# Where a kernel splits its tokens and stores them, and how it sums its last rows

## The chip, the cores and the metric

The kernel runs on one core of a Trainium2 chip. The metric is the device time of one execution in microseconds (us). Before the change it is 602.17 us, the median of three runs (601.52 to 602.39).

## What is computed

A sequence of 2048 tokens of 512 channels goes through two branches, and a gate per token mixes them.

```python
g = sigmoid((x * gate_w).sum(-1, keepdims=True))
a = ssm(x)                                    # long convolution per channel, plus x * D_skip
b = ((x @ w_gate) * (x @ w_up)) @ w_down      # bilinear GLU, 1792 hidden channels
out = g * a + (1 - g) * b
```

In `ssm` the convolution's kernel K (2048 values per channel) is a sum of 128 complex exponentials, made from the parameters; the reference then multiplies Fourier transforms of K and x.

## The kernel before, in words

**Precision.** The GLU's matmuls take operands in fp32r, a form of fp32 with fewer bits. So each operand is *split* into a high part (a cast on ScalarE) and a low part (what is left, a subtraction on VectorE), and each product is three matmuls: low by high, high by low, high by high (`THREE`, line 525). A split is `split` (411).

**GLU.** The 1792 hidden channels are 14 blocks f of 128, in four groups of 3, 3, 4 and 4 blocks (line 24). The 2048 tokens are four columns of 512. For each group the columns are run through: 0 to 3 in the first group, 3 to 0 in the second, and so on to and fro, so that the column at the turn stays in place (`glu`, 630). For a column and a block, `hidden` (543) makes two products of 512 tokens, `pg` and `pu`, each of 4 x 3 matmuls; ScalarE copies pg out as `h`, VectorE multiplies pu by it, and the result is split into `hh` and `hl`. For each of the column's four rows of 128 tokens, `down` (570) then multiplies by the down weights (`dhi`, `dlo`) of the group's blocks into a bank `y`, of which there are two; `evacuate` (581) copies y out, scaled by 1 - g, and writes it to the output in the first group or adds it to the output by an accumulating DMA of GpSimd in the later ones.

**Tokens.** A column's tokens are four tiles `xs` of [128, 2, 512], high and low part, out of five buffers (`tokens`, 515). In the first group they are loaded unsplit into `raw` (two buffers, which the weights go through too, in a fixed order of turns), split into xs (ScalarE and VectorE), and stored split, 512 KB a tile, to `xs_d` in device memory. In the second, third and fourth group each column after the first is loaded from `xs_d`, 512 KB a tile. The column at the turn isn't loaded.

**Weights.** The first group's weights are split by ScalarE and VectorE, as are the down weights of the last. Of the others the high part is cast, and the low part is made by a negated copy and an accumulating DMA from the source (`rest`, 431).

**Convolution.** In 16 blocks of 32 channels, VectorE and ScalarE make tables of complex powers, and one step on TensorE (`k_block`, 1014, written `k<-v,x` in the trace) makes K of these channels from them. After every four blocks, a quarter q of the channels is transformed (`transforms`, 1312): two steps `k<-kt,w1k_t`, then for four parts T a second step (`m_second`, 1131) and a product on VectorE (`m_product`), after each two of them an inverse step (`m_inverse`, 1189), and at last `m_last` (1231, `k<-in,w_t` or `k<-x,w_t`). Between these steps the data go through device memory (`su_d`, `sk_d`, `y_d`). The transform of u (`u_part`, 664) and the gate come at the start, with a load of 1 MB of u for each of four parts.

**The end.** Rows of column 0 come last in the last group. Their output so far is loaded once into `sums` (tile kt in the trace). `ends` (599) adds for each of the four rows g times the convolution (two small operations, for the last two quarters of the channels), then the evacuated y, and stores the row with 256 KB. The fourth row's y goes to a buffer of raw instead of acc, so that four rows have room.

**Order.** The functions don't issue: they add tasks with an engine, an estimated length, what they read and write, and a rank. `Work.run` (263) then goes through all tasks as a planner: of those that can start it takes the one with the earliest start, then the lowest rank, with a model of engines and of one memory bus (300 bytes a ns). The instructions are issued on each engine in this order, for the whole kernel, and each engine works strictly in it. Nearly all instructions have the line of the planner's issuing helper, L119, in the profile.

Of the kernel before, what the change touches and what calls it, by code (L numbers as in the profile page):

```python
# [14 lines left out]
ALU = mybir.AluOpType  # L15
# [3 lines left out]
P = 128  # L19
L, D, N, F = 2048, 512, 128, 1792  # L20
KT = D // P
# [4 lines left out]
LAST = 3 if len(GROUPS) % 2 else 0  # L26
# [138 lines left out]
class Work:  # L165
# [27 lines left out]
    def add(self, engine, us, fn, r=(), w=(), rank=1, after=0.0, dma=0, hold=(), rows=(), many=0):  # L193


        task = Task(len(self.tasks), engine, us, fn, rank, after, dma)
        task.rows, task.many = rows, many
        self.tasks.append(task)
        clash = lambda p, q: p is None or q is None or p == q
        split = lambda x: x if isinstance(x, tuple) else (x, None)  # L200
        for tile, part in map(split, r):
            task.deps.update(t for p, t in tile.writers if clash(p, part))
        for tile, part in map(split, w):
            task.deps.update(t for p, t in tile.writers + tile.readers if clash(p, part))
        for tile, part in map(split, r):
            tile.readers.append((part, task))
        for tile, part in map(split, w):
            tile.writers.append((part, task))
        for tile, _ in map(split, [*r, *w, *hold]):
            if tile.pool and tile not in task.tiles:  # L210
                task.tiles.append(tile)
                tile.users.append(task)
        task.deps.discard(task)
        return task
# [105 lines left out]
def gated_mix_kernel(  # L320
# [16 lines left out]
    pe, dve, act, sp, pool_q = (InOrder(tc, e) for e in (nc.tensor, nc.vector, nc.scalar, nc.sync, nc.gpsimd))  # L337
    uv = u.rearrange("(p r) d -> p r d", r=NR)
    ov = out.rearrange("(p r) d -> p r d", r=NR)
    work = Work()  # L340
    add = work.add
# [12 lines left out]
    m_su, m_sk, m_y, m_out, m_xs, m_turn = (work.memory() for _ in range(6))  # L354
# [5 lines left out]
    def new(pool, tag, shape, dtype=F32, bufs=1, loose=False):  # L360
        return work.tile(pools[pool], tag, shape, dtype, bufs, loose)
# [14 lines left out]
    ngate = const.tile([P, NR], F32, name="ngate")  # L376
    m_gate = work.memory()
# [27 lines left out]
    def load(key, src, rank=0):  # L405
        if key in raws:
            return
        t = raws[key] = new("glu", "raw", [P, D], bufs=2)
        add("sp", 0.42, lambda: sp.dma_start(t.t, src), w=[t], dma=256, rank=rank)

    def split(hi, lo, s, key):

        t = raws[key]
        t, k = t if isinstance(t, tuple) else (t, None)
        src = lambda: t.t if k is None else t.t[:, k]
        got = t if k is None else (t, k)
        s, z = s if isinstance(s, tuple) else (s, s)
        ph, pl = (hi, s), (lo, z)
        at = lambda x, s: x.t if s is None else x.t[:, s] if hi is lo else x.t[:, s * D : (s + 1) * D]
        add("act", 0.62, lambda: act.copy(at(hi, s), src()), r=[got], w=[ph], rank=0)  # L420
        add(
            "dve", 0.69,
            lambda: dve.tensor_tensor(out=at(lo, z), in0=src(), in1=at(hi, s).bitcast(F32), op=ALU.subtract),
            r=[got, ph], w=[pl], rank=0,
        )
# [49 lines left out]
    def weights(fs):  # L475
        for f in fs:
            ws[f] = [new("glu", n, [P, 2 * D], F32R, SLOTS) for n in ("whi", "wlo")]
            if f == 0:
                for kt in range(KT):
                    first_split(kt)  # L480
                    if kt + 1 < KT:
                        tokens(0, 0, kt + 1)
                continue
            for c in range(2):
                load(("w", f, c), wts[f][:, c * D : (c + 1) * D])
                if f in GROUPS[0]:
                    split(*ws[f], c, ("w", f, c))
                else:
                    high(ws[f][0], c, ("w", f, c))
            if f not in GROUPS[0]:  # L490
                rest(*ws[f], wts[f][:, : 2 * D], 2)
# [23 lines left out]
    def tokens(gi, ci, kt):  # L515

        x = xs[kt] = new("glu", "xs", [P, 2, D], F32R, 5)
        if gi:
            add("sp", 0.42, lambda: sp.dma_start(x.t.bitcast(F32), xs_d[ci, kt]), r=[(m_xs, (ci, kt))], w=[x], dma=512, rank=0)
            return  # L520
        load(("x", gi, ci, kt), xT[kt * P : (kt + 1) * P, ci * D : (ci + 1) * D])
        split(x, x, (0, 1), ("x", gi, ci, kt))
        add("sp", 0.42, lambda: sp.dma_start(xs_d[ci, kt], x.t.bitcast(F32)), r=[x], w=[(m_xs, (ci, kt))], dma=512, rank=2)

    THREE = ((1, 0), (0, 1), (0, 0))
# [53 lines left out]
    ending = []  # L579

    def evacuate(gi, ci, r, y):
        t = 4 * ci + r
        final = gi == len(GROUPS) - 1 and ci == LAST
        acc = new("glu", "raw", [P, D], bufs=2) if final and r == 3 else new("glu", "acc", [P, D], bufs=3)
        add(
            "act", 0.69, lambda: act.activation(acc.t, y.t, AF.Copy, scale=ngate[:, t : t + 1]),
            r=[y, (m_gate, ci)], w=[acc], rank=0,
        )
        if final:
            ending.append((r, acc))  # L590
        elif gi == 0:
            add("sp", 0.42, lambda: sp.dma_start(ov[:, t, :], acc.t), r=[acc], w=[(m_out, t)], dma=256)
        else:
            add(
                "pool", 0.95, lambda: pool_q.dma_start(ov[:, t, :], acc.t, accum_op=ALU.add),
                r=[acc, (m_out, t)], dma=640, rows=[t],
            )

    def ends():

        t0 = 4 * LAST
        sums = new("tab", "kt", [P, 4, D])
        add(
            "sp", 0.42, lambda: sp.dma_start(sums.t, ov[:, t0 : t0 + 4, :]),
            r=[(m_y, (KT - 1, 0))], w=[sums, *((m_out, t0 + r) for r in range(4))], dma=1024, rows=range(t0, t0 + 4),
        )
        for r, acc in ending:
            t = t0 + r
            for q, (fin, parts) in late["fin"].items():
                add(  # L610
                    "dve", 0.25,
                    lambda r=r, q=q, t=t, fin=fin: dve.scalar_tensor_tensor(
                        sums.t[:, r, P * q : P * q + P], fin.t[:, 4 * (LAST % 2) + r], gate[:, t : t + 1],
                        sums.t[:, r, P * q : P * q + P], op0=ALU.mult, op1=ALU.add,
                    ),
                    r=[*parts, (m_gate, LAST)], w=[(sums, (r, q))], rank=0,
                )
            add(
                "dve", 0.69,
                lambda r=r, acc=acc: dve.tensor_tensor(  # L620
                    out=sums.t[:, r], in0=acc.t, in1=sums.t[:, r], op=ALU.add
                ),
                r=[acc], w=[(sums, (r, q)) for q in range(KT - 2, KT)], rank=0,
            )
            add(
                "sp", 0.42, lambda r=r, t=t: sp.dma_start(ov[:, t, :], sums.t[:, r]), r=[(sums, (r, q)) for q in range(KT - 2, KT)], w=[(m_out, t)],
                dma=256, rank=-1,
            )

    def glu():  # L630
        order = [(gi, ci) for gi in range(len(GROUPS)) for ci in (range(4) if gi % 2 == 0 else range(3, -1, -1))]
        tokens(0, 0, 0)
        weights(GROUPS[0])
        down_weights(GROUPS[0])
# [728 lines left out]
    for b in range(NB):  # L1363
# [10 lines left out]
        if b % 4 == 3:  # L1374
            transforms(b // 4)
    ends()

    work.run()
# [53 lines left out]
```

## Time and profile before

| | |
|---|---|
| median of three runs | 602.17 us |
| profiled execution | 601.78 us |
| its span, first to last instruction | 600.0 us |
| TensorE busy | 585.8 us |
| VectorE busy | 512.3 us |
| ScalarE busy | 401.0 us |
| moved by DMA | 137.33 MB |

The profile is of one execution. Busy time of TensorE counts a matmul from its start to its modelled end, and matmuls overlap, so a busy TensorE need not be at its peak. In a row of a time line come the start in us, the length in us, engine, line, operation, tile written <- tiles read, shape, count, and in brackets the idle time of the engine before it with what ended it. PE is TensorE, DVE VectorE, ACT ScalarE, POOL GpSimd, SP SyncE; SPq is the queue on which SyncE issues DMAs. In a row of a group stand the busy time and the mean ns of one, then the idle time before. In a row of DMA issues stand the count, the KB of each and the median us to landing. In a row of waits stand the total us, the number of times, and the longest.

### The profile page before, as it was taken

To read this page: it belongs to the slowest core of one execution; us is meant where nothing else is said; L and a number is where in the kernel's file an instruction comes from. 1 tells how busy PE (TensorE), PEld (TensorE's weight loads), DVE (VectorE), ACT (ScalarE), POOL (GpSimd) and SP (SyncE) were. 2 spreads that over 40 slices of the span, in tenths; PEclk is the share of its full clock that TensorE was granted. 3 is DMA by queue.
4 is the path that set the end of the run, shared out by engine and by line. 5 is a ranking of instruction groups with operands and counts; after the bars stand their busy time and mean duration, and the time that the engine had idled before them with its cause. 6 is when DMAs were issued, how large, how long until landed. Compare 5 with 4: busy or idle time off the path is not lost.

```text
span 600.0 us, 15878 instructions
## 1 busy us (share of the span) xinstructions
PE 585.8 (98%) x6500; PEld 443.4 (74%) x6500; DVE 512.3 (85%) x811; ACT 401.0 (67%) x893; POOL 128.9 (21%) x191
## 2 busy tenths in 40 slices
PE   8899999999999999999999999999999999999996
PEld 5657777777877787887777877866878777767674
DVE  6999999999998997999999999978999933486525
ACT  5279787999678479967959764979984423433522
POOL 0011212221204131310133301104353023201111
PEclk9989999999999999999999999999999999999998
DMA  8899979699869699996959945999999569959976
GB/s 276 314 357 340 336 281 338 187 207 253 232 175 227 166 241 248 195 229 163 302 135 266 215 129 171 226 250 239 182 203 260 95 159 355 244 153 264 279 141 122
DMA packets 71867, 137.33 MB, mean 229 GB/s; under 512 B 7156, under 2 KB 35828, under 8 KB 69364
## 3 DMA queue, kind: packets, MB, share of 16 engines
q1 hardware_dynamic: 47476, 88.21, 45.9%
q0 software_dynamic: 23904, 47.98, 40.4%
q8 instruction: 51, 0.84, 0.6%
q10 hardware_dynamic: 416, 0.13, 0.1%
q14 instruction: 20, 0.16, 0.1%
HBM read 81.25 MB, written 55.05 MB: 227 GB/s over the span
## 4 chain that ended last, share of the span: by engine, by line
PE 79%; DVE 8%; ACT 6%; DMA 5%; issue 1%; ACTq 0%; DVEq 0%
PE y L119 22%; PE pu L119 21%; PE pg L119 21%; PE k L119 15%; DMA raw<-in_wts 4%; DVE x L119 2%; DVE y L119 1%; DVE v L119 1%; ACT ts L119 1%; ACT whi L119 1%; DMA y<-in_xT 1%; ACT L119 1%; DVE h L119 1%; DVE t L119 1%; DVE xs L119 1%
## 5 line engine op out<-in xcount | busy, mean ns | idle before, releaser
L119 PE MATMUL pg<-xs,whi 128*128 128x512 f32 x448 | 139.2, 392 | 1.0 <-DVE xs L119 0.7
L119 PE MATMUL pu<-xs,whi 128*128 128x512 f32 x448 | 138.7, 391 | 0.0
L119 PEld LDWEIGHTS pg<-xs,whi 128*128 128x128 f32 x448 | 84.5, 189 | 20.0 <-ACT whi L119 2.0
L119 PEld LDWEIGHTS pu<-xs,whi 128*128 128x128 f32 x448 | 84.4, 188 | 17.1
L119 PE MATMUL y<-dhi,hl 128*128 128x512 f32 x224 | 90.5, 404 | 2.2 <-DVE x L119 1.1
L119 PE MATMUL pu<-xs,wlo 128*128 128x512 f32 x224 | 90.1, 402 | 0.9 <-issue 0.5
L119 PE MATMUL pg<-xs,wlo 128*128 128x512 f32 x224 | 90.1, 402 | 0.8 <-ACT whi L119 0.5
L119 PE MATMUL y<-dlo,hh 128*128 128x512 f32 x224 | 87.5, 391 | 1.3 <-DVE dlo L119 1.3
L119 PE MATMUL y<-dhi,hh 128*128 128x512 f32 x224 | 87.4, 390 | 0.0
L119 POOL DMA_DIRECT2D out<-acc x44 | 38.4, 954 | 184.8 <-ACT acc L119 173.8
L119 ACT COPY ev<-k 128x512 f32<-128x512 f32 x112 | 59.2, 595 | 15.7 <-PE k L119 15.6
L119 ACT CAST hh<-h 128x512 fp32r<-128x512 f32 x56 | 34.7, 620 | 43.3 <-DVE h L119 43.2
L119 ACT ACTIVATE acc<-y,ngate 128x512 f32<-128x512 f32 x63 | 42.8, 686 | 30.6 <-PE y L119 28.2
L119 DVE TENSOR_TENSOR h<-pu,h 128x512 f32<-128x512 f32 x56 | 38.6, 689 | 23.0 <-PE pu L119 22.2
L119 PEld LDWEIGHTS y<-dhi,hl 128*128 128x128 f32 x224 | 42.0, 188 | 21.7 <-issue 6.2
L119 PEld LDWEIGHTS pu<-xs,wlo 128*128 128x128 f32 x224 | 42.1, 188 | 19.2 <-issue 9.8
L119 PEld LDWEIGHTS pg<-xs,wlo 128*128 128x128 f32 x224 | 42.0, 188 | 19.1 <-issue 6.8
L119 ACT COPY h<-pg 128x512 f32<-128x512 f32 x56 | 33.1, 590 | 29.7 <-PE pg L119 27.8
L119 PEld LDWEIGHTS y<-dlo,hh 128*128 128x128 f32 x224 | 42.1, 188 | 9.5 <-DVE dlo L119 1.7
L119 PEld LDWEIGHTS y<-dhi,hh 128*128 128x128 f32 x224 | 42.1, 188 | 9.1
L119 DVE TENSOR_TENSOR hl<-h,hh 128x512 fp32r<-128x512 f32 x56 | 38.5, 687 | 8.4 <-ACT hh L119 8.4
L119 POOL DMA_DIRECT2D su_d<-ev x32 | 17.3, 549 | 90.2 <-ACT ev L119 90.2
(127 smaller groups left out, 1015.7 us busy)
## 6 DMA issues: line engine op xcount, KB each, us to landing
xs<-xs_d SPq DMA_DIRECT2D x36, 512.0 KB, 7.8
out<-acc POOLq DMA_DIRECT2D x44, 256.0 KB, 7.1
raw<-in_wts SPq DMA_DIRECT2D x36, 256.0 KB, 5.2
xs_d<-xs SPq DMA_DIRECT2D x16, 512.0 KB, 7.1
su_d<-ev POOLq DMA_DIRECT2D x32, 256.0 KB, 5.3
y_d<-ts SPq DMA_DIRECT2D x14, 512.0 KB, 6.5
in<-su_d POOLq DMA_DIRECT2D x24, 256.0 KB, 8.4
sk_d<-ev SPq DMA_DIRECT2D x6, 1024.0 KB, 6.2
```

Source lines behind the costliest of these rows:

```text
L119: got = getattr(self.engine, name)(*args, **kw)
```

## The change

Two edits. First, `tokens`: in the first group only column 3 is stored split. Columns 2, 1 and 0 are loaded unsplit again in the second group, split once more, and stored to `xs_d` there; column 3 isn't loaded in the second group, as it is the one at the turn. The third and fourth group read `xs_d` as before. In Python `gi > (ci < 3)` is `gi > 1` for columns 0 to 2 and `gi > 0` for column 3.

Second, the end: of the last column's four rows, the last two are not copied out of PSUM by ScalarE. Their bank y is read by the final sum on VectorE, which scales it by 1 - g in the same operation. The first two rows' sum is the same operation with a scale of 1.0. The fourth row's sum and store are cut into halves of 256 channels, the second half stored on ScalarE's queue. The convolution's share lies in the second half, and the parts that the planner knows are named accordingly.

```diff
@@ tokens
-        if gi:
+        if gi > (ci < 3):
             add("sp", 0.42, lambda: sp.dma_start(x.t.bitcast(F32), xs_d[ci, kt]), ...)
             return
         load(("x", gi, ci, kt), xT[kt * P : (kt + 1) * P, ci * D : (ci + 1) * D])
         split(x, x, (0, 1), ("x", gi, ci, kt))
+        if gi == 0 and ci < 3:
+            return
         add("sp", 0.42, lambda: sp.dma_start(xs_d[ci, kt], x.t.bitcast(F32)), ..., dma=512, rank=2)
@@ evacuate
-        acc = new("glu", "raw", [P, D], bufs=2) if final and r == 3 else new("glu", "acc", [P, D], bufs=3)
+        if final and r > 1:
+            ending.append((r, y))
+            return
+        acc = new("glu", "acc", [P, D], bufs=3)
@@ ends
-                    r=[*parts, (m_gate, LAST)], w=[(sums, (r, q))], rank=0,
+                    r=[*parts, (m_gate, LAST)], w=[(sums, (r, 1))], rank=0,
                 )
-            add(
-                "dve", 0.69,
-                lambda r=r, acc=acc: dve.tensor_tensor(
-                    out=sums.t[:, r], in0=acc.t, in1=sums.t[:, r], op=ALU.add
-                ),
-                r=[acc], w=[(sums, (r, q)) for q in range(KT - 2, KT)], rank=0,
-            )
-            add(
-                "sp", 0.42, lambda r=r, t=t: sp.dma_start(ov[:, t, :], sums.t[:, r]), ...
-                dma=256, rank=-1,
-            )
+            for n, cs in enumerate((slice(0, D // 2), slice(D // 2, D)) if r == 3 else (slice(0, D),)):
+                part = [(sums, (r, k)) for k in (range(2) if r < 3 else (n,))]
+
+                def total(r=r, t=t, acc=acc, cs=cs):
+                    scale = 1.0 if r < 2 else ngate[:, t : t + 1]
+                    dve.scalar_tensor_tensor(
+                        sums.t[:, r, cs], acc.t[:, cs], scale, sums.t[:, r, cs], op0=ALU.mult, op1=ALU.add
+                    )
+
+                add("dve", 0.42 if r == 3 else 0.69, total, r=[acc, (m_gate, LAST)], w=part, rank=0)
+                e, q = ("act", act) if n else ("sp", sp)
+                add(
+                    e, 0.42, lambda r=r, t=t, cs=cs, q=q: q.dma_start(ov[:, t, cs], sums.t[:, r, cs]), r=part,
+                    dma=128 if r == 3 else 256, rank=-1,
+                )
```

More of the change, by code (lines that the diff above doesn't have):

```diff
@@ L615, in ends @@
                     ),
-                    r=[*parts, (m_gate, LAST)], w=[(sums, (r, q))], rank=0,
+                    r=[*parts, (m_gate, LAST)], w=[(sums, (r, 1))], rank=0,
                 )
-            add(
-                "dve", 0.69,
-                lambda r=r, acc=acc: dve.tensor_tensor(
-                    out=sums.t[:, r], in0=acc.t, in1=sums.t[:, r], op=ALU.add
-                ),
-                r=[acc], w=[(sums, (r, q)) for q in range(KT - 2, KT)], rank=0,
-            )
-            add(
-                "sp", 0.42, lambda r=r, t=t: sp.dma_start(ov[:, t, :], sums.t[:, r]), r=[(sums, (r, q)) for q in range(KT - 2, KT)], w=[(m_out, t)],
-                dma=256, rank=-1,
-            )
+            for n, cs in enumerate((slice(0, D // 2), slice(D // 2, D)) if r == 3 else (slice(0, D),)):
[11 more added lines that the diff above has]
+                )
     def glu():
```

## The prediction

> **What bounds the kernel now.** I read the page first, then the busy time by stage (stages cut at 30, 45, 105, 225, 405 and 480 us), then the time line of the stages with loss, and last the waits and the transfers.
>
> ```profile
> span 600.0 us, 15878 instructions
> ...
> PE 585.8 (98%) x6500; PEld 443.4 (74%) x6500; DVE 512.3 (85%) x811; ACT 401.0 (67%) x893; POOL 128.9 (21%) x191
> ```
>
> ```profile
> core 0: us, PE busy (x) PEld busy (x) DVE busy (x) ACT busy (x) POOL busy (x), PEclk, DMA share, GB/s
> 0.00:15.00 15.00, 12.64 (x41) 8.17 (x42) 9.95 (x32) 8.90 (x16) 0.96 (x25) 1.00 0.85 276
> 15.00:30.00 15.00, 12.61 (x55) 9.90 (x54) 14.39 (x31) 4.18 (x7) 0.00 (x0) 1.00 0.84 314
> 30.00:45.00 15.00, 13.88 (x71) 8.12 (x69) 14.95 (x30) 11.01 (x38) 1.97 (x4) 0.89 0.96 356
> 45.00:105.00 60.00, 59.82 (x430) 44.13 (x431) 58.79 (x104) 48.45 (x104) 13.18 (x25) 1.00 0.89 324
> 105.00:225.00 120.00, 119.27 (x1325) 93.15 (x1328) 114.68 (x172) 94.13 (x216) 29.67 (x39) 1.00 0.84 211
> 225.00:405.00 180.00, 179.84 (x2303) 138.25 (x2286) 168.21 (x245) 138.00 (x305) 35.60 (x43) 1.00 0.87 211
> 405.00:480.00 75.00, 74.30 (x874) 57.93 (x875) 72.35 (x110) 54.90 (x128) 24.99 (x31) 1.00 0.92 196
> 480.00:600.00 120.00, 113.46 (x1428) 83.75 (x1426) 59.00 (x96) 41.46 (x83) 22.51 (x26) 0.99 0.86 215
> ```
>
> Two things are to be seen. TensorE is full from 45 to 585 us, so only what it loses before and after can be had: 2.4 us in the first row, 2.39 in 15 to 30, 1.12 in 30 to 45 (where the granted clock is 0.89, worth 15 x 0.11 = 1.65 us more), and some 5.7 behind its last matmul. And VectorE is as full until 480 (98% from 15 to 105, 96% from 105 to 225), with the tables of the convolution's kernel; then it is half idle. So there are two streams: the GLU on TensorE, and the convolution, paced by VectorE until 480 and by hops over memory after. Whichever ends last sets the time.
>
> The loss of 15 to 45, in the time line of TensorE, ScalarE and VectorE:
>
> ```profile
> 27.07 0.51 PE L119 MATMUL y<-dhi,hl 128*128 128x512 f32 x1 [1.05 <-DVE x L119]
> 28.92 0.50 PE L119 MATMUL y<-dlo,hh 128*128 128x512 f32 x1 [1.34 <-DVE dlo L119]
> ...
> 30.20 0.63 PE L119 MATMUL pg<-xs,wlo 128*128 128x512 f32 x1
> ```
>
> ```profile
> 26.40 0.62 ACT L119 CAST dhi<-raw 128x512 fp32r<-128x512 f32 x1 [1.24 <-DMA raw<-in_wts]
> ...
> 28.18 0.68 DVE L119 TENSOR_TENSOR dlo<-raw,dhi 128x512 fp32r<-128x512 f32 x1
> ```
>
> The page puts the first stall on VectorE, but the matmul needs dhi, whose cast ended at 27.02; the cast had waited for a load. On SyncE's queue, and in the transfers of 9 to 31 us:
>
> ```profile
> 9.79 3.76 SPq L119 DMA_DIRECT2D xs_d<-xs  x4
> 13.98 0.51 SPq L119 DMA_DIRECT2D in<-in_u  x1
> ...
> 16.77 0.58 SPq L119 DMA_DIRECT2D raw<-in_wts  x1
> ```
>
> ```profile
> raw<-in_wts SPq DMA_DIRECT2D x1, 256.0 KB, 9.6
> ...
> raw<-in_wts SPq DMA_DIRECT2D x36, 256.0 KB, 5.2
> ```
>
> That load took 9.6 us against a median of 5.2 (last row, whole run), behind four stores of xs, the first column's, and the 1 MB of u. Both stalls hang on it.
>
> **The change part by part.** *Stores out of the first group.* Of 16 stores of 512 KB, 12 leave group 0. The four at 9.79 are 2.1 MB, 6.7 us at the 314 GB/s of the second row. Without them u goes out 3.76 us sooner and the third dhi load, which can't issue before its slot is free at 16.77, lands near 16.8 + 5.2 = 22 instead of 26.4. Then the 2.39 us of 15 to 30 go, and I take the half-speed stretch behind them to go too (1.65). The 1.12 of 30 to 45 stay: VectorE is full there (14.95 of 15), and its splits of the second column's tokens are late next. Gain 4.0; bounds 0 (VectorE's order holds dlo back whatever lands) and 2.39 + 1.12 + 1.65 = 5.2. The other eight stores lie between 30 and 96 us, where TensorE loses 0.2 in 60: nothing.
>
> The Trainium skill ("TensorE: Matmul & The Clock Gate", Part 1) has the clock fall to half after an idle window of about 3.4 us. Here it was at half (0.63 for a matmul of 0.39) after gaps of 1.05 and 1.34, less than that. By the page one short gap left over would cost no clock, and the 1.65 come back whole; by the trace a part of them would stay, and the gain be about 3.2.
>
> *Splits and stores in the second group.* There 12 loads of 512 KB become 12 of 256 KB with a split each, and 12 stores of 512 KB are added: 3.1 MB more on DMA engines busy 0.84. The durations are those of group 0:
>
> ```profile
> L119 DVE TENSOR_TENSOR xs<-raw,xs 128x512 fp32r<-128x512 f32 x12 | 8.1, 685 | 0.2 <-ACT xs L119 0.2
> ...
> L119 ACT CAST xs<-raw 128x512 fp32r<-128x512 f32 x12 | 7.3, 620 | 1.2 <-DMA raw<-in_xT 0.6 <-PE pu L119 0.5
> ```
>
> ```profile
> xs<-xs_d SPq DMA_DIRECT2D x36, 512.0 KB, 7.8
> ...
> raw<-in_xT SPq DMA_DIRECT2D x12, 256.0 KB, 5.7
> ```
>
> Tokens come as soon as before (5.7 + 0.62 + 0.69 = 7.0 against 7.8), so TensorE waits for none. ScalarE takes 7.3 us in a stage where it is busy 94 of 120: nothing. But the wait for a free xs slot, which stood on SyncE, now stands on ScalarE, with the hh casts and VectorE's split queued behind it; TensorE's waits of this kind are 0.7 us now and I leave them. SyncE gets 12 stores, each waiting for a split, ahead of other loads; the third group first reads them columns later. The raw buffers (two, in fixed order) now serve 12 tokens ahead of group 2's weights, whose first two loads came early until now. Late weights would cost what the late dhi costs in 25 to 30 us (2.39); but a whole column of matmuls is still to run when the last token has been split, against a load of 5.2 and a cast of 0.62, so I take nothing.
>
> VectorE is where it costs: 8.1 us in a stage with 5.3 idle, ahead of tables that are late anyway. Bounds: 0 (all goes into idle time) and 8.1. Its idle time of this kind:
>
> ```profile
> DVE h L119 <- PE pu L119: 4.3, 5, 3.5
> ...
> DVE h L119 <- PE pu L119: 1.9, 5, 0.7
> ```
>
> These are its waits for the GLU in 130 to 260 and 260 to 480 us: 6.2. With the GLU 4.0 earlier and VectorE later they close, so the tables slip 8.1 - 6.2 = 1.9. That is what I take.
>
> *What a slip does to the end.* TensorE's last step that needs a table (k<-v,x), the convolution's last loads, its last step, and the sums:
>
> ```profile
> 481.17 2.07 PE L119 MATMUL k<-v,x 128*32 128x64 f32 x128
> ...
> 573.28 2.15 SPq L119 DMA_DIRECT2D x<-y_d  x4
> ...
> 583.22 1.09 PE L119 MATMUL k<-x,w_t 64*32 64x512 f32 x16
> ...
> 592.38 0.69 DVE L119 TENSOR_TENSOR kt<-acc,kt 128x512 f32<-128x512 f32 x1 [0.49 <-ACT acc L119]
> ...
> 594.38 0.69 ACT L119 ACTIVATE raw<-y,ngate 128x512 f32<-128x512 f32 x1 [2.03 <-PE y L119]
> 595.10 0.69 DVE L119 TENSOR_TENSOR kt<-raw,kt 128x512 f32<-128x512 f32 x1 [2.02 <-ACT raw L119]
> ```
>
> ```profile
> x<-y_d SPq DMA_DIRECT2D x4, 256.0 KB, 5.6
> ...
> out<-kt SPq DMA_DIRECT2D x1, 256.0 KB, 2.8
> ```
>
> The last of the four loads, issued near 575.0, is in at 575.0 + 5.6 = 580.6; its last step runs at 583.22, in TensorE's order. From there to 595.79 are 12.6 us, of which VectorE waited 2.5 for y: 10.1 of work, and 4.2 to the end of the span (2.8 until the store has landed, the rest closing). So the convolution alone would end at 580.6 + 10.1 + 4.2 = 594.9, plus the slip.
>
> *The last rows.* Before: copy from PSUM (0.69), sum (0.69), a 256 KB store. After: two half sums from PSUM, the second store on ScalarE's queue.
>
> ```profile
> L119 DVE TENSOR_TENSOR kt<-k,kt 128x256 f32<-128x256 f32 x32 | 13.4, 419 | 4.5 <-ACT kt L119 4.4
> ...
> L119 DVE SCALAR_TENSOR_TENSOR v<-v 128x256 f32<-128x256 f32 x16 | 10.1, 631 | 0.0
> ```
>
> A half costs 0.42 (a sum from PSUM of that size), at most 0.63; the second ends at 594.36 + 0.84 = 595.2 (at most 595.6) instead of 595.79, the first at 594.8. No row has a store of 128 KB at the end: it lands no sooner than the 256 KB (2.8), or in proportion to its bytes (1.4 sooner); I take 0.2 of that, near the first. Gain 0.6 + 0.2 = 0.8, bounds 0.2 and 0.6 + 1.4 = 2.0. Rows 0 and 1 change a sum for one with a scale of 1.0 at the same length; row 2 loses a copy that nothing waits for. ScalarE has nothing left then that its store could hold up.
>
> The Trainium skill ("DMA: Bandwidth & Descriptors") gives a fixed 2.0 us and bytes over 436 GB/s per transfer; by it half a store saves an estimated 0.3, and the gain would be 0.9. No row here has both sizes on an idle bus.
>
> **Sum.** GLU: 600.0 - 4.0 - 0.8 = 595.2. Convolution: 594.9 + 1.9 = 596.8. The later sets the span: 596.8. The profiled execution took 601.78 with a span of 600.0; with the same 1.78 around it, 598.6. That is 0.5% under its own time and 0.6% under the median of 602.17.
>
> **Rivals.**
> *VectorE's whole 8.1 us reach the end* (other side). For it: 96 to 98% busy until 480, and after its last table the convolution is a row of hops with little slack. Against: 5.3 + 11.8 + 2.7 = 19.8 us of idle time between 105 and 480. Then 594.9 + 8.1 = 603.0, a time of 604.8. It decides from a slip of about 5: there the convolution ends at 600 again.
> *The first loss stays*: the order written for VectorE, full from 15 to 45, still sets the second column. For it: 14.39 and 14.95 of 15 us busy, and dlo split 1.2 us after its cast was done. Against: VectorE's order is planned with the loads' times, and a token that lands sooner can be split sooner. The tail alone: 599.2, a time of 601.0, if the slip stays under 4.
> *No slip at all*: the GLU's end decides, 595.2, a time of 597.0. With the gains at their bounds the convolution is last, at 594.9, or 593.5 with a last store that lands 1.4 sooner: 595.3.
>
> **Chances.** Forecast 0.45, spanning 597.3 to 601; no slip 0.12; first loss stays 0.14; full slip 0.29. A measurement of this kernel can tell about 0.2% (1.2 us) from no change: faster is under 601.0. Faster 0.57 (the first two), within 0.2% 0.13, slower 0.30. The range goes from the third rival's lower bound, 595.3, to 605.5, a little above the full slip.
>
> **What would show it.** Right: no wait over 1 us on TensorE between 25 and 30 us, the third dhi load landing in about 5 us, a granted clock of 1.00 in 30 to 45; VectorE at 98% in 105 to 225 with 12 more xs splits; the last k<-v,x (481.17 now) about 2 us later; the last store issued under 0.9 us after the last matmul's end. Wrong: the last k<-v,x 5 or more later, TensorE waiting for x at the end, or stalls behind xs splits in 130 to 230. The order of work is planned anew for the whole kernel, so any engine may be given other neighbours than I assume; that would make every term wrong together.

## The result, and the profile after

The changed kernel takes 617.09 us (median of four runs, 614.60 to 621.19) against 601.85 (601.17 to 602.39) for the kernel before beside it: a ratio of 1.026, 95% interval 1.020 to 1.032, or 15.2 us more. The forecast was 598.6 with a range to 605.5. The sign was wrong, and the time lies outside the range. Two single runs far above the others of their kernel (719.75 us of e2_tail and 1463.96 of e3_splits) are left out of the ratios below.

The profiled execution took 614.60 us, the shortest of the four. Its page, the span and TensorE's busy time first:

```profile
span 612.6 us, 15936 instructions
...
PE 587.2 (96%) x6500; PEld 444.4 (73%) x6500; DVE 520.0 (85%) x824; ACT 409.0 (67%) x905; POOL 129.6 (21%) x191
```

TensorE's span is its busy time and its idle time: 585.8 + 14.2 before, 587.2 + 25.4 now. So 11.2 of the 12.6 us are idle time, and the 1.4 of busy time are the same 6500 matmuls, at a mean granted clock of 0.991 instead of 0.994. The stages that the prediction cut, with the same columns:

```profile
15.00:30.00 15.00, 14.39 (x64) 11.37 (x63) 14.86 (x33) 6.56 (x12) 0.00 (x0) 1.00 0.59 181
30.00:45.00 15.00, 15.00 (x87) 10.34 (x86) 14.90 (x27) 11.89 (x37) 2.12 (x4) 1.00 0.88 307
45.00:105.00 60.00, 58.59 (x318) 42.08 (x317) 52.11 (x90) 51.02 (x107) 15.63 (x29) 1.00 0.81 274
105.00:225.00 120.00, 115.61 (x1223) 91.04 (x1222) 116.82 (x177) 90.29 (x199) 24.38 (x33) 1.00 0.77 211
225.00:405.00 180.00, 172.88 (x2416) 133.29 (x2415) 167.30 (x246) 133.64 (x310) 38.45 (x47) 0.98 0.87 205
405.00:480.00 75.00, 74.21 (x830) 56.08 (x829) 69.86 (x108) 60.32 (x137) 24.59 (x30) 1.00 1.00 228
480.00:613.00 133.00, 123.94 (x1532) 92.12 (x1531) 74.06 (x116) 46.36 (x93) 23.46 (x27) 0.98 0.80 202
```

The gain of the first 45 us is there: TensorE works 14.39 and 15.00 us where it worked 12.61 and 13.88, at a clock of 1.00. Then it loses in stages where it had lost under 1 us each: 1.2 us more in 45 to 105, 3.7 in 105 to 225, 7.0 in 225 to 405; and 2.1 more behind 480. The stages of the two kernels don't hold quite the same work, so this says where TensorE stood idle and not at what. And VectorE, 58.79 of 60 us busy in 45 to 105 before, is now idle there for 7.9.

What TensorE waited for, in the view of waits (total, times, longest):

```profile
PE k L119 <- DVE y L119: 3.5, 1, 3.5
PE y L119 <- DVE hl L119: 3.4, 3, 1.7
PE k L119 <- issue: 3.3, 2, 1.9
PE pg L119 <- ACT h L119: 2.2, 2, 1.4
PE k L119 <- DVE v L119: 2.0, 1, 2.0
```

There is no one wait that explains the loss; there are many of 1 to 3.5 us, each for another tile, GLU and convolution mixed. The longest is the first of these lines of TensorE's time line. It costs 3.5 us of waiting, and then the matmuls take 0.63 instead of 0.39 until 281.7:

```profile
274.74 2.19 PE L119 MATMUL k<-y,w3s 32*64 32x128 f32 x64 [3.51 <-DVE y L119]
276.86 0.80 PE L119 MATMUL pg<-xs,wlo 128*128 128x512 f32 x1
...
280.86 0.58 PE L119 MATMUL pu<-xs,wlo 128*128 128x512 f32 x1
...
281.74 0.39 PE L119 MATMUL pu<-xs,wlo 128*128 128x512 f32 x1
```

The steps that need a table, first and last k<-v,x (the view of tile v by stretches; after the shortest, median and longest matmul in ns stand the first and last start). Before, the first:

```profile
L119 PE MATMUL k<-v,x x128: 219/219/243, 97.0 to 98.8; 128*32 128x64 f32 x128
```

After, the first and the last:

```profile
L119 PE MATMUL k<-v,x x128: 219/219/243, 107.0 to 108.9; 128*32 128x64 f32 x128
...
L119 PE MATMUL k<-v,x x128: 219/219/243, 503.1 to 504.9; 128*32 128x64 f32 x128
```

The last came at 481.17 before: it is 22 us late, 10 of which arose in the first group, before a token is split anew (the first such split starts at 133.0). The prediction had named this sign ("5 or more later"). Another of its signs, a stall behind splits of xs in 130 to 230, shows once: TensorE waits 1.73 us for hl at 144.82, and ahead of the cast hh that hl is made from stand two casts of xs in ScalarE's order (from 140.20).

The end, on VectorE, on ScalarE's queue, and the transfers from 590 us on (KB each, us to landing):

```profile
606.00 0.88 DVE L119 SCALAR_TENSOR_TENSOR kt<-y,ngate,kt 128x256 f32<-128x256 f32 x2 [1.12 <-PE y L119]
```

```profile
606.91 0.35 ACTq L119 DMA_DIRECT2D out<-kt  x1
```

```profile
out<-x POOLq DMA_DIRECT2D x1, 256.0 KB, 7.7
out<-kt SPq DMA_DIRECT2D x1, 128.0 KB, 4.6
out<-kt ACTq DMA_DIRECT2D x1, 128.0 KB, 4.4
```

The two half sums take 0.88, as forecast, and the last store is issued 0.9 us after the last matmul's end. But a half store lands in 4.4 us, where the whole one took 2.8 in the kernel before.

### The profile page after: what moved, and what is told of

It is laid out like the page before. It is cut to its first block, busy times and chain, and to the rows that moved or that the text cites. A ratio compares the mean times of both kernels' runs of the same rounds, so it can differ in the third digit from the quotient of the medians.

```text
span 612.6 us, 15936 instructions
## 1 busy us (share of the span) xinstructions
PE 587.2 (96%) x6500; PEld 444.4 (73%) x6500; DVE 520.0 (85%) x824; ACT 409.0 (67%) x905; POOL 129.6 (21%) x191
## 4 chain that ended last, share of the span: by engine, by line
PE 51%; DVE 16%; issue 15%; DMA 10%; ACT 4%; POOL 3%; SPq 0%; DVEq 0%; POOLq 0%; ACTq 0%
PE pg L119 14%; PE y L119 13%; PE pu L119 13%; PE k L119 11%; DVE v L119 3%; DMA in<-sk_d 3%; DVE x L119 3%; DMA raw<-in_wts 2%; DVE y L119 2%; DMA out<-acc 2%; DVE h L119 2%; DMA su_d<-ev 1%; DVE m L119 1%; DMA xs_d<-xs 1%; DVE xs L119 1%
## 5 line engine op out<-in xcount | busy, mean ns | idle before, releaser
L119 PE MATMUL pg<-xs,wlo 128*128 128x512 f32 x224 | 91.4, 408 | 2.7 <-ACT h L119 2.2
L119 PEld LDWEIGHTS k<-v,x 128*32 128x32 f32 x2048 | 30.5, 109 | 7.7 <-issue 6.7
```

The costliest lines, as they stand in the source:

```text
L119: got = getattr(self.engine, name)(*args, **kw)
```

## The experiments

All times are medians beside the kernel before on the same chip (601.6 to 602.6 us, by the call). The theories are *order* (the loss is the order that was planned anew for the whole kernel), *VectorE* (the loss is the price of the new splits), and *GLU ahead* (without the stores the GLU runs ahead and takes VectorE from the tables). In the first expectations theory A is VectorE and theory B is GLU ahead.

### The edits one by one

**e1_tokens**: the first edit alone.

```diff
-        if gi:
+        if gi > (ci < 3):
...
+        if gi == 0 and ci < 3:
+            return
```

> The first edit alone (columns 2, 1 and 0 split anew and stored in the second group), with the end as before. Both theories below put the whole loss on this edit: 613 to 618 us, within 1% of the changed kernel. If the end had a part in it (its last stores landed 4.4 to 4.6 us after they went out in the changed kernel's profile, against 2.8), this run is 1 us faster than the changed kernel.

Measured 619.41 us, ratio 1.027 (1.024 to 1.031). The loss is the first edit's.

**e2_tail**: the second edit alone (the other hunks of the diff).

> The second edit alone (last two rows summed from PSUM, the last in halves), tokens as before. By the prediction 0.8 us faster than before, 601.0. By the changed kernel's profile (6.6 us from the last matmul's end to the end of the span, 5.6 before) 1 us slower, 602.8.

Measured 601.92, ratio 0.9988 (0.9976 to 1.0001): -0.7 us, not clear of zero.

**e3_splits**: the tokens split anew in the second group, all stores left in the first.

```diff
-        if gi:
+        if gi > 1:
...
+        if gi:
+            return
```

> The three columns are split anew in the second group, but they are stored in the first as before, so the first group does what it did. Theory A (VectorE's 8.1 us of new splits, put into a full stage, are the loss): the whole loss is here, 612 to 617. Theory B (without the stores the GLU runs ahead in the first group, VectorE does the GLU's work first and the tables come late): the tables of the first group stay in time (first k<-v,x near 97 us, not 107), and the time is 602 to 608.

Measured 616.69, ratio 1.023 (1.021 to 1.025), with the first k<-v,x at 97.0. Taken alone, that is what theory VectorE expected.

**e4_nostore**: the 12 stores gone, nothing added.

```diff
-            add("sp", 0.42, lambda: sp.dma_start(x.t.bitcast(F32), xs_d[ci, kt]), r=[(m_xs, (ci, kt))], w=[x], dma=512, rank=0)
+            add("sp", 0.42, lambda: sp.dma_start(x.t.bitcast(F32), xs_d[3, kt]), r=[(m_xs, (3, kt))], w=[x], dma=512, rank=0)
...
+        if ci < 3:
+            return
```

> Leaves out the 12 stores of columns 0 to 2; the later groups read column 3's tokens in their place (same bytes, wrong columns). No new splits. Theory A: only the gain is left, 596 to 599. Theory B: the first k<-v,x comes 5 to 10 us late (102 to 107 against 97) and the time is 602 to 608 in spite of less work.

Measured 608.91, ratio 1.010 (1.009 to 1.012). This kernel does *less* than the kernel before, and is 6.3 us slower, with the first k<-v,x at 103.9: close to what GLU ahead expected. And the parts don't add up: 14.1 (e3) and 6.3 (e4) stand against 16.8 for e1. A fixed price per instruction gives neither; this is where the order came under suspicion.

### The order held, the work changed

**e5_nostore_old_order**: as e4, but the planner still counts the 12 stores, so every engine keeps the order of the kernel before.

```diff
-        add("sp", 0.42, lambda: sp.dma_start(xs_d[ci, kt], x.t.bitcast(F32)), r=[x], w=[(m_xs, (ci, kt))], dma=512, rank=2)
+        add("sp", 0.42, lambda: ci == 3 and sp.dma_start(xs_d[ci, kt], x.t.bitcast(F32)), r=[x], w=[(m_xs, (ci, kt))], dma=512, rank=2)
```

> As e4_nostore (the 12 stores of columns 0 to 2 left out, later groups load column 3's tokens in their place, so the output is not the reference's), but the planner still counts the 12 stores, so that every engine keeps the order of the kernel before and only the stores' transfers are gone. Theory order (the loss of 6.3 us in e4 is the order that was planned anew): 598 to 601, faster than 602.2 by part of the 4.0 us that the prediction gave to the first load, and the first k<-v,x stays near 97 us. Theory GLU ahead (without the stores' traffic the GLU's work itself takes VectorE from the tables, whatever the order): about 608 again, first k<-v,x near 104.

Measured 602.66, ratio 1.0002 (0.9984 to 1.0021). The 6.3 us of e4 are gone with its order, and the first k<-v,x stands at 96.8 again (103.9 in e4); GLU ahead fell. But the 4.0 us of the prediction's first step did not come either. The third load of dhi landed 3.9 us after its issue instead of 9.6. ScalarE, VectorE and TensorE in this kernel:

```profile
24.94 0.61 ACT L119 CAST dhi<-raw 128x512 fp32r<-128x512 f32 x1
```

```profile
28.05 0.69 DVE L119 TENSOR_TENSOR dlo<-raw,dhi 128x512 fp32r<-128x512 f32 x1
```

```profile
28.79 0.50 PE L119 MATMUL y<-dlo,hh 128*128 128x512 f32 x1 [1.87 <-DVE dlo L119]
...
33.28 0.50 PE L119 MATMUL y<-dhi,hl 128*128 128x512 f32 x1 [1.68 <-ACT acc L119]
```

The cast is 1.46 us earlier (26.40 before), yet VectorE makes dlo at 28.05 (28.18 before), because it works without a pause through what stands ahead of it in its order. TensorE waits 0.57 us for hl and 1.87 for dlo, 2.44 in all against 2.39 before, and then 1.68 (0.55 before) for a copy of y.

**e9_splits_old_order**: the price of the new splits put into the order of before by hand. Each of the second group's 12 token loads is followed by a cast on ScalarE and an operation of 128x512 on VectorE, in place.

```diff
+            if gi == 1 and ci < 3:
+                hi, lo = (lambda: x.t[:, 0].bitcast(F32)), (lambda: x.t[:, 1].bitcast(F32))
+                t.later = [
+                    (0.0, lambda: act.copy(x.t[:, 0], hi())),
+                    (0.7, lambda: dve.tensor_tensor(out=x.t[:, 1], in0=lo(), in1=lo(), op=ALU.max)),
+                ]
...
+        late = sorted(((t.end + us, n, fn) for t in order for n, (us, fn) in enumerate(t.later)), key=lambda e: e[:2])
         for t in order:
+            while late and late[0][0] <= t.start:
+                late.pop(0)[2]()
             t.fn()
```

> The kernel before in its own order, with the price of the new splits put into it by hand: behind each of the second group's 12 loads of xs a cast of its high half on ScalarE (12 x 0.62 us) and an operation of the same size as a low half on VectorE (12 x 0.69 = 8.2 us), both in place, where the split would stand. All else, stores and the order of all other instructions, is as before. Theory VectorE (these 8 us are what the change costs): 610 to 617. Theory order: the splits themselves cost what the prediction's step gave them at most, 602 to 605, last k<-v,x up to 8 us later than 481.

Measured 606.07, ratio 1.0076 (1.0061 to 1.0091): +4.5 us, 1 us over what theory order allowed and 4 under the least of theory VectorE. TensorE's last table step, TensorE's waits for tables between 100 and 260 us, and for VectorE a row of its time line and a row of its waits in the same window:

```profile
484.34 2.07 PE L119 MATMUL k<-v,x 128*32 128x64 f32 x128
```

```profile
PE k L119 <- DVE v L119: 1.7, 3, 1.0
```

```profile
243.09 0.69 DVE L119 TENSOR_TENSOR h<-pu,h 128x512 f32<-128x512 f32 x1 [2.69 <-ACT ev L119]
```

```profile
DVE h L119 <- ACT ev L119: 2.7, 1, 2.7
```

In the kernel before, the same views say, with the same operation h<-pu in the time line:

```profile
PE k L119 <- DVE v L119: 0.3, 1, 0.3
```

```profile
239.48 0.69 DVE L119 TENSOR_TENSOR h<-pu,h 128x512 f32<-128x512 f32 x1 [3.50 <-PE pu L119]
```

```profile
DVE h L119 <- PE pu L119: 4.3, 5, 3.5
```

The profile gives the wait of e9 to a copy of ScalarE, but pu's last matmul ends only at 242.99, 0.1 us before h<-pu starts, as it does in the kernel before (239.37). So VectorE's longest wait for pu did not close: it shrank from 3.50 to 2.69, because pu itself came 3.6 us later. The tables slip by 3.2 us. TensorE waits for them in the second group, and the GLU's matmuls stand behind in the same order: between 105 and 225 TensorE is busy 2.7 us less than before (116.60 of 120 against 119.27), 1.7 of its waits there are for tables and 0.8 for a copy of y, and the last matmul of the kernel starts at 597.40 instead of 593.95.

**e10_edit_old_order**: as e9, with the 12 stores moved into the second group.

```diff
+                    (1.5, lambda: sp.dma_start(xs_d[ci, kt], x.t.bitcast(F32))),
...
-        add("sp", 0.42, lambda: sp.dma_start(xs_d[ci, kt], x.t.bitcast(F32)), r=[x], w=[(m_xs, (ci, kt))], dma=512, rank=2)
+        add("sp", 0.42, lambda: ci == 3 and sp.dma_start(xs_d[ci, kt], x.t.bitcast(F32)), r=[x], w=[(m_xs, (ci, kt))], dma=512, rank=2)
```

> As e9_splits_old_order, and the 12 stores moved as the change moves them: the first group issues none of them, the second group stores each tile 0.8 us after its split. The second group loads column 3's tokens in place of its own, so the output is not the reference's. This is the first edit's work in the order of the kernel before, less the turns in raw and with 3.1 MB more to load. Theory order: within 2 us of e9_splits_old_order, 601 to 606. Theory VectorE or stores: 612 or more, as e1_tokens (619).

Measured 606.92, ratio 1.0089 (1.0072 to 1.0106): +5.3 us. The interval overlaps that of e9, so the moved stores cost nothing that can be told. This is the first edit's work at the same places of the same order (less the turns in raw), and it costs a third of the 16.8 of e1_tokens. Here the profile names the wait between 100 and 260 us by pu again:

```profile
DVE h L119 <- PE pu L119: 3.0, 1, 3.0
```

The stages show the difference to the changed kernel, too. From 225 to 405 us, where the edit adds no work, TensorE is busy 180.0 of 180 us in this kernel and 172.88 in the changed one.

### The work held, the order changed

**e6_before_u20_5, e7_before_d31, e12_before_u22, e13_before_u18, e15_before_u21**: the kernel before, not one instruction more or less, with one of the planner's constants changed.

```diff
-U_STEP = 20.0
+U_STEP = 20.5
```

(22.0, 18.0 and 21.0 in e12, e13 and e15; in e7 the assumed DMA_RATE is 0.31 instead of 0.3.)

> The kernel before with the planner's step between the due times of u's tiles 20.5 in place of 20.0: the same instructions, another order, neither edit of the change. Theory order: several us of loss in new short stalls of TensorE, 605 to 612. Theory VectorE (only the added or moved work counts): 602 within 1.

> The kernel before with the planner's assumed DMA rate 0.31 in place of 0.30: the same instructions, another order, neither edit of the change. Theory order: 604 to 612, with TensorE's idle time above the 14.2 us of before by most of the difference. Theory VectorE: 602 within 1.

> The kernel before with the step between u's due times 22.0, as in e8_after_u22, which took 612.4: the same planner's setting on both sides. Theory order: this one is no longer the faster of the two by 15 us; 608 to 620, the difference to 612.4 of either sign. Theory VectorE: 602 within 2.

> The kernel before with the step between u's due times 18.0. Theory order: 606 to 618, as with 20.5 (616.7) and 22.0 (610.3). Theory VectorE: 602 within 2.

> The kernel before with the step 21.0. Theory order: 606 to 618. Theory VectorE: 602 within 2.

**e8_after_u22, e14_after_u18, e16_after_u21, e11_after_dma2**: the changed kernel with the same steps, and once with 2 us more until a transfer counts as landed.

```diff
-                t.end = bus + 0.5
+                t.end = bus + 2.5
```

> The changed kernel with the step between the due times of u's tiles 22.0 in place of 20.0: all of the change's instructions, another order. Theory order: the loss of 15 us moves by several us with nothing else changed, 603 to 612. Theory VectorE (8.1 us of new splits and the late tables cost it, whatever the order): within 3 us of 617.

> The changed kernel with the step 18.0. If the change has a price of its own of 4 to 5 us (the 5.3 of e10 less the 0.7 of the last rows) and the order the rest, it stands 0 to 9 us above e13_before_u18 and may be faster than 617. If the change itself costs 15 us, 15 above it.

> The changed kernel with the step 21.0. Price of its own 4 to 5 us: 0 to 9 us above e15_before_u21. The change itself costs 15: 15 above it.

> The changed kernel, whose planner counts 2 us more until a transfer has landed: the same instructions in an order that leaves more room for late loads. If TensorE's stalls come from transfers later than planned, they go: 604 to 612. If any other order is about as bad as another: 610 to 620.

| planner | kernel before, us (ratio, interval) | changed kernel, us (ratio, interval) |
|---|---|---|
| step 18 | 604.19 (1.005, 1.003 to 1.008) | 617.70 (1.026, 1.020 to 1.031) |
| step 20 | 601.85 (1) | 617.09 (1.026, 1.020 to 1.032) |
| step 20.5 | 616.67 (1.024, 1.021 to 1.027) | not run |
| step 21 | 601.51 (0.9995, 0.998 to 1.001) | 611.51 (1.017, 1.013 to 1.021) |
| step 22 | 610.27 (1.015, 1.013 to 1.017) | 612.42 (1.017, 1.015 to 1.019) |
| rate 0.31 | 616.06 (1.022, 1.020 to 1.025) | not run |
| landing + 2 | not run | 617.63 (1.027, 1.022 to 1.032) |

The ratios are to the kernel before at step 20. A new order alone, for the same instructions, costs anything from nothing to 14.4 us (616.67 against 602.23 beside it): nearly as much as the whole change. At 22 the two kernels can't be told apart by these intervals. More room for transfers (e11) doesn't cure it. My expectations of the pairs, 0 to 9 us apart, missed at 18 (13.5) and narrowly at 21 (10.0). Of the expectations of theory order for the kernel before, e6 and e7 came out above theirs, e12 inside, e13 below (604.19), and e15 (601.51) is what theory VectorE said: a new order can cost much, and need not.

How an order alone loses time, in e6_before_u20_5. Its page, ScalarE, TensorE, and the transfers of 115 to 140 us:

```profile
span 616.7 us, 15875 instructions
...
PE 592.7 (96%) x6500; PEld 447.4 (73%) x6500; DVE 512.9 (83%) x811; ACT 402.0 (65%) x893; POOL 129.2 (21%) x191
```

```profile
139.84 0.69 ACT L119 ACTIVATE acc<-y,ngate 128x512 f32<-128x512 f32 x1 [4.77 <-DMA out<-acc]
141.07 0.62 ACT L119 CAST dhi<-raw 128x512 fp32r<-128x512 f32 x1 [0.54 <-DMA raw<-in_wts]
141.59 0.58 ACT L119 COPY h<-pg 128x512 f32<-128x512 f32 x1
```

```profile
142.22 0.80 PE L119 MATMUL pg<-xs,wlo 128*128 128x512 f32 x1 [5.51 <-ACT h L119]
142.82 1.05 PE L119 MATMUL pg<-xs,whi 128*128 128x512 f32 x2
...
146.05 0.39 PE L119 MATMUL pg<-xs,wlo 128*128 128x512 f32 x1
```

```profile
out<-acc SPq DMA_DIRECT2D x3, 256.0 KB, 13.3
```

A copy of y needs an acc buffer that a store to memory still reads; three such stores take 13.3 us here (median). ScalarE waits 4.77 us for it, and behind it in its order stand a cast and the copy h<-pg, which frees the bank pg. TensorE waits 5.51 for that bank, and then runs at half clock until 146.0. In the kernel before ScalarE waits for no store of this kind between 115 and 145 us. The Trainium skill ("PSUM — Partial Sum Buffer", Engine vs sequencer instructions) calls the queues of ScalarE and VectorE strict first-in first-out, with matmuls starting in program order; the rows agree: pg was complete by 136.7, when TensorE fell idle, and h<-pg started at 141.59, after the copy and the cast ahead of it.

### Does it hold in another order?

**e17_tail_u21**: the second edit alone, with step 21.

```diff
-U_STEP = 20.0
+U_STEP = 21.0
```

> The second edit alone (last rows from PSUM, the last in halves) with the step 21.0, the best setting of the kernel before so far (e15_before_u21, 601.5). If the tail's gain of e2_tail (0.7 us) holds in this order too: 600.8, under both kernels. If it is lost to the order: 601.5 or more.

Measured 602.50, ratio 1.0007 (0.9994 to 1.0019): no gain in this order. So nothing here beats the kernel before by more than can be told.

**e18_edit_order_u21**: e10 with step 21, the edit's work put into the order that the unedited kernel gets there.

> As e10_edit_old_order (the first edit's work put by hand into the order of the unedited kernel; the second group loads column 3's tokens, so the output is not the reference's), in the order that the step 21.0 gives. If the work has a price of its own of about 5 us in any good order: 605.5 to 608, against 611.5 of e16_after_u21, whose order was planned with the edits in it. If e10's 5.3 us were this one order's luck: under 604 or over 610.

Measured 605.51, ratio 1.0064 (1.0042 to 1.0086): 3.5 us over the median of the kernel before beside it (3.9 by the ratio), 4.0 over e15. So a price of about 4 to 5 us holds in a second order, where the changed kernel, planned anew, takes 611.51. From 225 to 405 us TensorE is busy 180.0 of 180 us here as well, and 174.44 in e16.

## Why the prediction was wrong, point by point

**The step that failed** is the one that the sum rests on without pricing it: every edit was costed at its place in the order of before, though "the order of work is planned anew for the whole kernel". The prediction named that in its last sentence and gave it no term, no bound and no rival. It is worth about two thirds of the result: of +15.2 us, the first edit's work takes 5.3 (e10) and the last rows give 0.7 (e2), so 15.2 - 5.3 + 0.7 = 10.6 came with the order planned anew (what the turns in raw cost is in it, as e10 leaves them out). That an order alone can do this is shown by e6, e7 and e12; that the change does without it when the order is held, by e10 and e18.

**Stores out of the first group (-4.0).** The local signs came as named: no wait over 1 us between 25 and 30, the third dhi load in 3.8 us, a clock of 1.00. The value did not. With the order held, the earlier load is worth nothing (e5): the lower bound, with its reason, "VectorE's order holds dlo back whatever lands". The stall stood on a load in the profile, but removing the load only uncovered VectorE, full from 15 to 45. With the order planned anew, TensorE does gain those 3 us, and e4, which has the gain and no added work, still ends 6.3 us later: the new order loses more behind it. Whether the gain would reach the end in a good order isn't shown.

**Splits (+1.9 of 8.1).** The waits for pu that were to close, 6.2 us, hardly did, with the order held: between 100 and 260 us they went from 4.3 to 2.7 (e9) or 3.0 (e10), and between 260 and 480 from 1.9 to 2.2, because pu came later as well. The splits were cheaper than their price, as VectorE's busy time grew by 6.5 us (512.3 to 518.8 in both) and not by 8.1. Together the tables slip by 3.2, not 1.9. The place was wrong as well: the prediction let the slip reach only the convolution, which had 5 us in hand, so that a slip of 3 would have been free. In fact TensorE works through one order that holds both streams; it waits for late tables (1.7 us in e9, 0.3 before), and the GLU behind them is late too (3.45 us at the last matmul, with the other short waits). "Whichever ends last sets the time" was the wrong sum. The rival with the whole 8.1 us, 604.8, came closest to e10, by another path.

**Costs at nothing.** SyncE's moved stores: e10 against e9 bears that out. ScalarE's casts went in together with VectorE's work, and no run parts the two. Late weights: the changed kernel's waits have no row for them above 0.9 us, two waits for whi that the kernel before has too; in e3 TensorE stood idle for 4.2 us before a matmul that reads dlo (428.32; the profile names no releaser), so another order can bring such a wait.

**The end (-0.8).** e2 gives -0.7, but its interval reaches zero and e17 gives nothing, so that the number fits is luck: in the profile of e2 the time from the last matmul's end to the end of the span is 5.6 us, 0.1 less than before, and in the changed kernel it is 6.6. The halves' sums were right (0.44 each). The landing was wrong: 3.3 us in e2 and 4.4 in the changed kernel against 2.8 for the whole row before, so half a row landed later than a whole one, where the prediction took it to land 0.2 sooner. An accumulating transfer of x was under way beside the last stores in all three, and no run shows what made the difference. What the sums save, the landing takes back.

**What stays open.** Whether an order exists in which the changed kernel takes the 606 that its work would cost. Four planned orders and one with other landing times gave 611.5 to 617.7, six of the kernel before 601.5 to 616.7. The first table step isn't the tell-tale: it came at 107.0 in the changed kernel but at 95.9 in e8, which still took 612.4. Nor is the last: in e6, at 616.67 us, it is 3.3 us late. The turns in raw were not tried alone: ScalarE waits for the second group's unsplit tokens 0.7 us in the changed kernel, but 3.9 to 4.5 in e8, e14 and e16, so they may cost something themselves, or make good orders rarer.

## What to carry to other kernels

When a planner writes one fixed order for all engines, an edit is two changes: its work, and a new order; run the unchanged kernel with a planner constant moved a little before pricing the work, because that spread (here 0 to 14.4 us) is what a new order alone can do, and a difference inside it says little about the edit's work. Price an edit by putting its instructions into the old order by hand. And two streams that share one engine with a fixed order have little slack of their own: here a late table of one stream held up the matmuls of the other that stood behind it.

## What the runs showed of the hardware

**Half clock came in steps of 3.41 us, and not after every set of short gaps.** In the kernel before, gaps of 1.05 and 1.34 us near 27 to 29 us were followed by half clock from 30.15 to 33.57. In e5, at the same matmuls, gaps of 0.57 and 1.87 and then 1.68 were not:

```profile
30.00:45.00 15.00, 12.61 (x71) 7.36 (x70) 14.97 (x29) 11.24 (x38) 2.19 (x4) 1.00 0.70 243
```

TensorE does the same 71 matmuls in this stage as before, in 12.61 busy us instead of 13.88, and waits for the rest. The Trainium skill ("TensorE: Matmul & The Clock Gate", Part 1) describes a free-running activity window, so that the cost varies from run to run; these two runs agree with that, though its idle window of about 3.4 us is longer than any of these gaps.

The granted clock, read in stretches of 0.1 us, shows a grid. In e6 it falls to half at 29.77, 46.84, 139.00 and 569.08 us, for 3.41, 3.41, 6.83 and 6.83 us, and these starts are 5, 27 and 126 times 3.41 us apart. Counted in steps of such a grid, laid through the falls of each trace, seven traces (before, changed, e3, e5, e6, e7, e14) agree: while the clock was full, it fell after every step in which TensorE was busy for less than 1.5 of the 3.41 us and after none with more than 1.74; in between both happened. In the kernel before, the step from 26.74 holds the end of the first gap and all of the second, and was busy for 1.74. In e5 (whose clock falls once, at 597.32, behind its last matmul) the edges at 27.29 and 30.71 part the three gaps: the steps were busy for 2.47, 1.92 and 1.73, and the clock stayed full. So in these traces a gap cost clock by how much of one step was idle, not by its own length.

**Some orders spread more from run to run**: 614.6 to 621.2 us for the changed kernel and 613.4 to 620.6 for e14, but also 603.2 to 610.5 for e13, which has the instructions of the kernel before; that kernel itself gave 600.7 to 604.6 in 18 runs, and the changed kernel at step 22 (e8) 611.7 to 613.2 in four. So the spread goes with some of the orders and not with the change as such. Why isn't shown.
